# Gated recurrence and low-rank mixer: a half-word sign step, the second chunk's gates by a ratio, and a re-planned order

## The chip, the cores and the metric

One Trainium2 chip, one core. The metric is the device time of one execution in microseconds (us); lower is better. The kernel before was timed in three runs: 546.83, 547.58 and 550.12 us, median 547.58 us. Separately, one execution was profiled; it took 550.73 us, and the durations quoted below come from that one.

## What is computed

Two blocks follow each other. The first is a recurrence with complex gates over 768 steps, for 4 batches and 8 heads of 48 channels; the second is a mixer over the 384 columns that the heads make together. Cut to what matters:

```python
mag = np.sqrt(a_re * a_re + a_im * a_im)
scale = np.minimum(mag, 0.999) / (mag + 1e-06)
a_re_n, a_im_n = (a_re * scale, a_im * scale)
for t in range(S):
    ar, ai = (a_re_n[:, :, t, :, None], a_im_n[:, :, t, :, None])
    new_re = ar * S_re - ai * S_im
    new_im = ar * S_im + ai * S_re
    kv = np.einsum('bhd,bhe->bhde', k[:, :, t], v[:, :, t])
    S_re, S_im = (new_re + kv, new_im)
    y[:, :, t] = np.einsum('bhd,bhde->bhe', q[:, :, t], S_re)

xt = x.transpose(0, 2, 1)               # x: y of all heads, 384 columns
u = x + (xt @ U @ V).transpose(0, 2, 1)
out = u + np.maximum(u @ w_ch1, 0.0) @ w_ch2
```

The four weight arrays (`U`, `V`, `w_ch1`, `w_ch2`) come as 64-bit floats; everything else is 32-bit. The kernel turns the weights into 32-bit floats itself.

## The kernel before, in words

**Tiling.** The 4 x 768 steps are 24 chunks of 128 steps. Chunks go in pairs, called groups, for the gates (12 groups) and for the mixer. The gates of a chunk become a log magnitude (`GL`) and an angle (`gate`, then `F`, in turns). A matmul with a triangle of ones sums them along the chunk (tile `es ps` for magnitudes, `ph` for angles); exponentials (`es`) and sines (`cs`) of the sums weigh `q` and `k` (`qk`, then `QKC`); transposes (`tr`), products (`inner`, `dk`, `y`) and a running state (`GM`, `G`) give the output of the chunk (`xo`). The mixer then takes `rank`, `mixed`, the first weight product (`up` for the first two pairs, `few` with fewer products for the others) and the second (`down`).

**Gates.** `magnitudes_of(lo, hi)` works on chunks lo to hi-1. The first group is done chunk by chunk (parts (0,1) and (1,2)), every other group as one part of two chunks. There are two ways. The long one squares both parts on ACT, adds the squares with a clamp (L660), keeps the larger square (L661), makes two checks of the angle's range into `bad` (L663), and takes the logarithm of the sum and, apart from that, of the larger square. The other, `ratio_of` (L685), takes the logarithm of the real part (after L689), its reciprocal by an exponential, the ratio of imaginary to real part, its square with the check `wide` (L693), and finds the log magnitude from the ratio (L697, L700). The angle comes from the ratio in both. Before, the test is on the group: `g >= RATIO` with `RATIO = 1`, so both chunks of group 0 take the long way.

**Weights.** `single` (L558) converts one piece of 128 x 768 weights: 12 such pieces and one of 384 columns (`U` and `V`). A piece lies in one of two `raw` buffers as pairs of 32-bit words. Five steps follow: the high word read as a float and scaled (into the weight tile), the low word scaled to an integer of three bits (into a `cx` buffer), a shift left by 3 (L589), an integer add of the two (L445, the group `w<-w,stage`), and the sign, ORed in from the high word by a two-operand step (L591). For the first six pieces all five are on DVE; for the later ones the two scalings are on ACT (L439, `w<-stage` and `stage<-stage`). `raw` and `cx` are both views of a tile named `stage` in the profile.

**Order.** Every operation is recorded in a plan. `ORDER` is a written-out list of operation numbers; the program is issued in that order, so each engine's queue and each DMA queue (SP's, POOL's) holds its own operations in the order of that list. `SPARE` puts matmuls on the identity ahead of named operations (L1421, L1425). An assertion demands that an operation comes after what it needs and that a buffer is free. Loads are issued by SP in that order too, so a load waits in SP's queue for its buffer and everything behind it waits too. At the end a flag is read, and where a check has failed a slow general version runs; it does not run with these inputs.

Lines L436, L439, L442 and L445 are helpers: table load, activation, multiply, add.

## Time and profile before

| | |
|---|---|
| three timed runs | 546.83, 547.58, 550.12 us (median 547.58) |
| the profiled execution, its own time | 550.73 us |
| its span, first to last instruction | 548.5 us |
| time outside the span | 2.2 us |
| ACT busy | 297.3 us (54%) |
| POOL busy | 32.0 us (6%) |
| moved by DMA | 39.92 MB, over half of it in the first 140 us |

PE is the matmul engine, PEld its weight loads, DVE, ACT and POOL the vector, scalar and general engines, SP the engine that issues most DMAs. A busy PE in this profile is one that has a matmul under way; ends of matmuls are modelled. A line of a group gives source line, engine, operation, tile written and read, shape, and count. The chain of waits is the chain of work that ended last, followed back from the last instruction.

### The profile page before, as it was taken

The numbers are of one execution on the slowest core, as the hardware profiler recorded it, in microseconds if no ns is written. First come the engines' busy times: TensorE is split into PE (matmuls) and PEld (weight loads), VectorE is DVE, ScalarE is ACT, GpSimd is POOL, SyncE is SP. The second block draws the span as 40 slices with busy tenths as digits, with TensorE's granted clock in tenths as the row PEclk, the third lists the DMA queues.
The fourth block names the chain that finished last, engine by engine and source line by source line (L and its number), as shares of the span: only waits on it lengthen the run. The fifth ranks groups of instructions, "written<-read, shape, count | busy, mean of one in ns | idle before, by whom it ended". The sixth has DMA issues, their size and how long they took to land.

```text
span 548.5 us, 16738 instructions
## 1 busy us (share of the span) xinstructions
PE 524.2 (96%) x7296; PEld 473.6 (86%) x7296; DVE 419.6 (77%) x819; ACT 297.3 (54%) x545; POOL 32.0 (6%) x61
## 2 busy tenths in 40 slices
PE   2889989999999999999999999999999999999996
PEld 1767776867899998999999889999999989999995
DVE  6999995999999987897896775788685635656452
ACT  6889986894586866657457644533654322011100
POOL 1000000000020001000101001000111000000020
PEclk9999997999999999999999999999999999999999
DMA  9689893753325550422343420220131000000021
GB/s 222 130 177 202 168 211 81 188 96 75 57 54 110 90 111 11 87 38 38 73 76 72 90 42 20 46 46 17 29 76 46 3 2 1 1 14 2 1 73 34
DMA packets 150688, 39.92 MB, mean 73 GB/s; under 512 B 145912, under 2 KB 147408, under 8 KB 150608
## 3 DMA queue, kind: packets, MB, share of 16 engines
q1 hardware_dynamic: 148400, 34.43, 32.1%
q0 software_dynamic: 2208, 4.35, 2.4%
q8 instruction: 59, 0.97, 0.8%
q14 instruction: 21, 0.17, 0.1%
HBM read 33.60 MB, written 4.76 MB: 70 GB/s over the span
## 4 chain that ended last, share of the span: by engine, by line
PE 82%; DVE 9%; ACT 4%; DMA 3%; issue 2%; SPq 0%; DVEq 0%; ACTq 0%; POOLq 0%
PE down L1270 28%; PE few L1138 23%; PE dk L895 4%; PE inner L875 4%; PE y L932 4%; PE tr L846 4%; PE y L924 2%; PE up L1026 2%; DMA gate<-F 2%; PE rank L968 2%; PE mixed L991 2%; ACT gate L439 1%; PE uTp L1009 1%; PE es ps L721 1%; PE es ps L725 1%
## 5 line engine op out<-in xcount | busy, mean ns | idle before, releaser
L1146 ACT COPY h<-few 128x512 f32<-128x512 f32 x60 | 34.7, 586 | 79.4 <-PE few L1138 79.2
L1270 PE MATMUL down<-w,h 128*128 128x192 f32 x396 | 72.6, 330 | 0.7 <-ACT h L439 0.7
L852 ACT COPY QK<-tr 112x512 f32<-112x512 f32 x96 | 51.4, 593 | 35.3 <-PE tr L846 35.2
L1270 PEld LDWEIGHTS down<-w,h 128*128 128x128 f32 x396 | 64.4, 190 | 2.9 <-ACT h L439 1.2
L445 DVE TENSOR_TENSOR xo<-down,xo 128x192 f32<-128x192 f32 (+1 forms) x79 | 29.9, 385 | 37.0 <-PE down L1270 36.7
L1138 PE MATMUL few<-extra,w 128*128 128x128 f32 x400 | 50.3, 276 | 0.0
L1138 PEld LDWEIGHTS few<-extra,w 128*128 128x128 f32 x400 | 47.7, 192 | 0.2
L445 DVE TENSOR_TENSOR h<-few,h 128x512 f32<-128x512 f32 x30 | 20.6, 689 | 34.5 <-PE few L1138 22.1
L439 ACT ACTIVATE gate<-gate 128x768 f32<-128x768 f32 (+1 forms) x52 | 40.7, 792 | 11.3 <-DVE wide L693 7.8
L1150 DVE CUSTOM_DVE_ANT_1 h<-few,h 128x512 f32<-128x512 f32 x60 | 39.7, 684 | 7.6 <-PE few L1138 7.1
L442 DVE TENSOR_TENSOR QKC<-qk,cs 128x768 f32<-128x768 f32 x48 | 44.8, 950 | 0.3
L1270 PE MATMUL down<-stage 128*128 128x192 f32 x198 | 38.4, 332 | 0.0
L1026 PE MATMUL up<-uT,w 128*128 128x256 f32 x144 | 35.5, 397 | 0.2 <-ACT extra L439 0.2
L1270 PEld LDWEIGHTS down<-stage 128*128 128x128 f32 x198 | 32.3, 190 | 2.2 <-issue 1.5
L1026 PEld LDWEIGHTS up<-uT,w 128*128 128x128 f32 x144 | 27.3, 195 | 6.5 <-ACT xo L943 1.2
L1138 PE MATMUL few<-gate,w 128*128 128x128 f32 x240 | 31.9, 277 | 0.0
L436 ACT ACT_TABLE_LOAD x24 | 30.8, 1283 | 1.1 <-PEq L1477 0.7
L1214 POOL DMA_DIRECT2D out_dram<-xo x32 | 19.6, 645 | 191.1 <-DVE xo L445 159.5
L771 POOL DMA_DIRECT2D gate<-F x15 | 12.1, 805 | 303.2 <-DVE F L794 166.2
L1138 PEld LDWEIGHTS few<-gate,w 128*128 128x128 f32 x240 | 29.2, 192 | 0.4 <-DVE gate L1110 0.2
L895 PE MATMUL dk<-VP,QKC 64*48 64x48 f32 (+1 forms) x1408 | 27.6, 217 | 1.1 <-issue 1.1
L846 PEld LDWEIGHTS tr<-ident,QKC 64*112 64x112 f32 x768 | 23.7, 130 | 5.5 <-issue 2.3
(166 smaller groups left out, 1089.3 us busy)
## 6 DMA issues: line engine op xcount, KB each, us to landing
stage<-in_moe_w_ch_dram SPq DMA_DIRECT2D x12, 768.0 KB, 4.7
gate<-in_a_re_dram SPq DMA_DIRECT2D x24, 192.0 KB, 4.6
gate<-in_a_im_dram SPq DMA_DIRECT2D x24, 192.0 KB, 3.4
qk<-in_k_dram SPq DMA_DIRECT2D x24, 192.0 KB, 4.8
qk<-in_q_dram SPq DMA_DIRECT2D x24, 192.0 KB, 3.1
VP<-in_v_dram SPq DMA_DIRECT2D x24, 192.0 KB, 4.5
out_dram<-xo POOLq DMA_DIRECT2D x12, 192.0 KB, 2.9
out_dram<-xo POOLq DMA_DIRECT2D x20, 96.0 KB, 2.2
```

The lines of the kernel that those rows point to most:

```text
L436: ACT(1.4, rank, lambda: nc.scalar.preload_act_table_set(name), writes=[TABLE])
L439: return nc.scalar.activation(out=o, in_=i, func=f, **kw)
L442: nc.vector.tensor_tensor(out=o, in0=a, in1=b, op=OP.mult)
L445: nc.vector.tensor_tensor(out=o, in0=a, in1=b, op=OP.add)
L846: nc.tensor.transpose(out=get(*ps[r])[0:DQ, h], in_=get(*qkc)[at, h].rearrange("p u d -> p (u d)")[:, 0:DQ], identity=ident[at, at], tile_ ...
L852: nc.scalar.copy(out=get(*QK)[:, u].rearrange("p (h t) -> p h t", t=CH)[:, :, r * HC:(r + 1) * HC], in_=get(*ps[r])[0:DQ])
L895: nc.tensor.matmul(out=get(*dk[r])[x:end, h], lhsT=get(*ks)[at, h, x // DP, 0:end - x], rhs=get(*VPi)[at, h], start=True, stop=True, tile_ ...
L1026: nc.tensor.matmul(out=get(*ps)[:, e], lhsT=w1[:, f, (ff + e) * 128:(ff + e + 1) * 128], rhs=get(*uT)[:, f], start=(f == 0), stop=(f == KD ...
L1138: nc.tensor.matmul(out=get(*ps)[:, q], lhsT=w()[:, q * 128:(q + 1) * 128], rhs=v[0](), start=(n == 0 and q == 0), stop=True, skip_group_ch ...
L1146: ACT(c_act(n3 * CH) - 0.045, RU, lambda i=i, k=k: nc.scalar.copy(out=at(i, k), in_=get(*ps)), [ps], [o])
L1150: DVE(c_dve(n3 * CH), RU, lambda i=i, k=k: nc.vector._custom_dve(dve_ops.TENSOR_ADD_SAT, out=at(i, k), in0=get(*ps), in1=at(i, k), s0=math ...
L1270: nc.tensor.matmul(out=get(*to)[:, part], lhsT=x(j), rhs=y[:, j], start=(first and j == 0), stop=(j == KH - 1), skip_group_check=not first)
```

## The change

Three things are changed, and nothing else.

**The sign of converted weights.** The two-operand step L591 is gone. In its place a one-operand step on 16-bit halves takes the top half of each high word, keeps its sign bit, and writes it to the upper half of the `cx` word. The low word's scaling writes the lower half of that word only. The integer add then brings in low bits and sign together. The step reads one half of every 8 bytes and writes one half of every 4.

```diff
-        for to_word, o_, i_, scale, at in ((False, lambda: o, lambda: hi().bitcast(FP), 2.0 ** -112, to),
-                                           (True, lambda: word(x()), lo, 2.0 ** -29, cx)):
+        limb = lambda a, u: a.bitcast(U16).rearrange("p (n u) -> p n u", u=2)[:, :, u]
+        top = lambda: get("raw", p)[:, 0:n].rearrange("p n two -> p (n two)").bitcast(U16).rearrange("p (n u) -> p n u", u=4)[:, :, 3]
+        for o_, i_, scale, at in ((lambda: o, lambda: hi().bitcast(FP), 2.0 ** -112, to), (lambda: limb(x(), 0), lo, 2.0 ** -29, cx + (0,))):
...
+        DVE(one, rank, lambda: nc.vector.tensor_scalar(out=limb(x(), 1), in0=top(), scalar1=0x8000, scalar2=None, op0=OP.bitwise_and),
+            [raw], [cx + (1,)])
         DVE(one, rank, lambda: nc.vector.tensor_scalar(out=b, in0=b, scalar1=3, scalar2=None, op0=OP.logical_shift_left), writes=[to])
         DVE(two, rank, lambda: add(word(o), word(o), word(x())), reads=[cx], writes=[to])
-        DVE(two, rank, lambda: nc.vector.scalar_tensor_tensor(out=b, in0=hi(), scalar=0x80000000, in1=b,
-                                                              op0=OP.bitwise_and, op1=OP.bitwise_or), reads=[raw], writes=[to])
```

**The second chunk's gates.** The test is on the part's first chunk, so chunk 1 takes `ratio_of`; chunk 0 alone keeps the long way, and `bad` has two columns fewer.

```diff
-    bad = singles.tile([128, 1 + 2 * GC], FP, name="bad")
+    bad = singles.tile([128, 1 + 2 * RATIO], FP, name="bad")
...
-            if g >= RATIO:
+            if lo >= RATIO:
                 ratio_of(lo, hi, t, R1, W, X, L, Y, AR, AI)
                 return
```

**The order.** `ORDER` is another list, of 2200 operations by a new numbering where there were 2203; the identity matmuls of `SPARE` keep their counts and their places (2, 10, 14 and 5). The multiset of PE, POOL and SP operations is the same in both kernels; their sequence is not. Lines of the changed kernel lie one or two lower than before (L591 is the new sign step there, L593 the shift).

## The prediction

> **What bounds the kernel now.** I read the totals first, then a table of busy time by stage, then the chain of waits, and only then single steps.

> ```profile
> span 548.5 us, 16738 instructions
> PE 524.2 (96%) x7296; PEld 473.6 (86%) x7296; DVE 419.6 (77%) x819; ACT 297.3 (54%) x545; POOL 32.0 (6%) x61
> ```

> PE is busy for 524.2 of 548.5 us, so at most 24.3 us of the span is time in which no matmul ran. The busy share alone does not say where that time lies; the table by stage does (columns: stretch, its length, busy us of PE, PEld, DVE, ACT, POOL with counts, granted PE clock, DMA share, GB/s).

> ```profile
> 0.00:20.00 20.00, 8.45 (x39) 6.10 (x40) 14.37 (x38) 13.46 (x25) 2.17 (x14) 1.00 0.90 204
> 20.00:40.00 20.00, 17.09 (x424) 14.40 (x422) 19.30 (x31) 18.08 (x33) 0.00 (x0) 1.00 0.74 150
> 40.00:60.00 20.00, 19.79 (x371) 15.64 (x365) 19.57 (x32) 18.91 (x34) 0.00 (x0) 1.00 0.90 199
> 60.00:80.00 20.00, 19.38 (x413) 15.28 (x413) 18.92 (x32) 19.38 (x35) 0.00 (x0) 1.00 1.03 199
> 80.00:100.00 20.00, 18.34 (x155) 12.38 (x155) 13.71 (x24) 13.85 (x24) 0.00 (x0) 0.83 0.48 121
> 100.00:120.00 20.00, 19.86 (x91) 14.28 (x90) 19.26 (x31) 16.88 (x27) 0.96 (x1) 1.00 0.69 140
> 120.00:140.00 20.00, 19.18 (x164) 13.98 (x163) 19.22 (x30) 11.29 (x18) 2.11 (x3) 1.00 0.42 78
> 200.00:250.00 50.00, 50.00 (x658) 45.64 (x653) 42.60 (x88) 31.61 (x59) 3.31 (x5) 1.00 0.24 46
> 500.00:548.00 48.00, 43.29 (x315) 42.59 (x313) 24.03 (x57) 3.88 (x8) 3.73 (x7) 0.98 0.09 31
> ```

> Three things are to be seen. From 140 us on PE has no gap worth naming (200 to 250 is full), and the last 4.7 us are the outputs leaving. Both parts of the change lie ahead of 140 us, where all weights are converted and the first gates made. There PE loses 11.55 us in the first 20 (it waits for the first gates), 2.91 in the next 20, then 0.21, 0.62, 1.66, 0.14 and 0.82. DVE is at 95 to 98% in the five stretches from 20 us on that have the full clock, ACT at 90 to 97% up to 80 us. So DVE work removed there is real, but PE has the same work as before, and only PE's gaps can be given back. What DVE saves beyond them is hidden behind PE.

> **The sign step.** Durations of one 128 x 768 step, and the pace of neighbours:

> ```profile
> L585 DVE TENSOR_SCALAR stage<-stage x6: 353/552/556, 12.1 to 56.5; 128x768 int32<-128x768 uint32 x5, 128x384 int32<-128x384 uint32 x1
> L589 DVE TENSOR_SCALAR w<-w 128x768 uint32<-128x768 uint32 x12 | 6.7, 554 | 2.9 <-ACT w L439 2.8
> L591 DVE SCALAR_TENSOR_TENSOR w<-stage,w x12: 948/954/967, 16.9 to 118.9; 128x768 uint32<-128x768 uint32 x12
> 12.05 0.55 DVE L585 TENSOR_SCALAR stage<-stage 128x768 int32<-128x768 uint32 x1
> 12.52 0.55 DVE L585 TENSOR_SCALAR w<-stage 128x768 f32<-128x768 f32 x1
> 118.00 1.82 DVE L591 SCALAR_TENSOR_TENSOR w<-stage,w 128x768 uint32<-128x768 uint32 x2
> SPq L572 <- DVE w L591: 26.9, 6, 9.2
> ```

> A two-operand step takes 0.954 us, a one-operand step 0.55; neighbours overlap, so what counts is the pace: 1.82 - 0.954 = 0.87 us against 12.52 - 12.05 = 0.47. Removed: 12 x 0.87 and one of 384 columns, about 0.47. Added: 12 x 0.47 and one of about 0.27. The saving on DVE is 10.9 - 5.9 = 5.0 us. No row shows a step that writes every other 16-bit half. Its bounds are the one-operand rows (0.47) and the two-operand row (0.87, no saving at all); below 0.47 I see no reason to go, since no row has a quicker step of 768 elements. I take 0.47, because L585 already reads one word of every 8 bytes and takes 0.552, the same as L589, which reads without gaps. The same doubt holds for the low word's scaling, which now writes halves: 0 to 0.4 us for each of the five whole pieces on DVE and 0.2 for the short one, 2.2 in all; I take 0.

> [...]

> The change also moves a buffer's release. SP's weight loads (L572) waited 26.9 us in all for L591, the last reader of `raw`. Now the last reader is the sign step, ahead of the integer add, and the loads start earlier, into a stretch where DMA is already at 0.90 to 1.03. PE is not waiting for these loads, so I count nothing; what it can do to PE is a rival.

> **The second chunk's gates.**

> ```profile
> 5.96 0.56 DVE L660 CUSTOM_DVE_ANT_0 GL<-gate 128x384 f32<-128x384 f32 x1 [0.23 <-ACT gate L439]
> 6.56 0.52 ACT L439 ACTIVATE GL<-GL 128x384 f32<-128x384 f32 x1 [0.62 <-DVE GL L660]
> 7.21 0.62 ACT L439 ACTIVATE gate<-GL,leps 128x384 f32<-128x384 f32 x1
> 7.86 0.36 DVE L671 TENSOR_SCALAR GL<-GL 128x384 f32<-128x384 f32 x1 [0.27 <-ACT gate L439]
> 11.11 0.56 DVE L445 TENSOR_TENSOR GL<-GL,gate 128x384 f32<-128x384 f32 x1 [0.25 <-ACT gate L439]
> 12.64 1.17 PE L725 MATMUL es ps<-GL,prefix_r 128*128 128x384 f32 x2
> 20.34 0.55 DVE L794 SCALAR_TENSOR_TENSOR F<-F,ph 128x384 f32<-128x384 f32 x1 [0.75 <-ACT F L439]
> 23.01 0.95 DVE L442 TENSOR_TENSOR qk<-qk,es 128x768 f32<-128x768 f32 x1
> 31.52 0.96 DVE L700 SCALAR_TENSOR_TENSOR GL<-GL,gate 128x768 f32<-128x768 f32 x1
> 32.62 1.53 PE L725 MATMUL es ps<-GL,prefix_r 128*128 128x384 f32 x4 [1.03 <-DVE GL L700]
> ```

> The ratio way has fewer steps but one long chain. Chunk 1's chain starts on DVE behind the step of 5.96, at about 6.43, and by these rows is 0.36 + 3 x 0.52 (logarithms) + 0.52 + 0.62 (exponentials) + 4 x 0.56 = 5.3 us; with ten hand-overs of 0.03 and some 0.3 for chunk 0's steps on the same engines it ends near 12.3. Before, the operand was there at 11.67, but its matmul started at 12.64, behind chunk 0's sum and the identity matmuls. So the longer chain is hidden, by 0.3 us; each us beyond that would move the table load, the angles and everything after by as much. Chunk 0's own add comes up to 0.3 us earlier, since two steps of chunk 1 no longer stand before it on DVE. ACT's new order (one more sine ahead of the second `F`) takes that back by 20.34. I count 0 here. Loads: the second half of `qk` for chunk 1 now stands behind two more gate loads and `VP`, some 0.6 MB, in SP's queue; 4.2 MB up to it at about 225 GB/s (204 over the first 20 us, which begin with 2 us of silence) lands near 20.6, 2.4 us ahead of its use at 23.01.

> **The other order.** From `F` at 20.34 to the end of L700 at 32.48 DVE is nearly full, and PE waits for that step (1.03 us at 32.62). Ahead of it the new order has one step of 0.47 less (L689, now before `F`), one sign of 0.87 less and one 384-column step of 0.27 less, and a shift and a `G` product of 0.47 each more: -0.7 us. The `G` product needs the totals, whose read-back now stands ahead of the next `qk` loads, so I add no wait.

> Then the small gaps: 0.21 + 0.62 + 0.14 + 0.82 = 1.79 us of PE in 40 to 80 and 100 to 140, while DVE is full and gets lighter. I take half: -0.9 us.

> One place gets tighter. From the third group of chunks on, an angle sum needs the previous `F` by way of a DMA that adds it:

> ```profile
> 125.37 1.11 PE L785 MATMUL ph<-GS,prefix_r 128*128 128x384 f32 x2
> 126.32 2.74 PE L1227 MATMUL down<-w,extra 128*128 128x384 f32 x8
> 128.99 1.14 PE L895 MATMUL dk<-VP,QKC 64*64 64x48 f32 x64
> 130.06 1.11 PE L846 MATMUL tr<-ident,QKC 64*112 64x64 f32 x32
> 131.10 2.86 PE L1026 MATMUL up<-uT,w 128*128 128x256 f32 x12
> 133.60 0.70 PE L785 MATMUL ph<-GS,prefix_r 128*128 128x384 f32 x2
> DMA to landing us min/median/max: 1.8/2.9/4.2
> ```

> Here 8.2 us lie between the two `ph`. In the new order half a block of `down` (1.3), three halves of a `tr` block (1.6), a block of `down` (2.6) and `dk` (1.1) lie between, with `ph` itself 7.4 us. If the chain still needs 8.2, PE waits 0.8; with the median landing, 1.1 us under the longest, it does not. I take +0.3.

> The sum: -0.7 - 0.9 + 0.3 = -1.3 us. The profiled execution (550.73: span 548.5 and 2.2 around it) would become 549.4; it stands 3.15 us above the median of the timed runs, and the same 1.3 us off 547.58 gives **546.3 us**.

> **The rivals.** The low clock in 80 to 100:

> ```profile
> 81.67 0.66 PE L924 MATMUL y<-VP,AT 64*64 64x48 f32 x11 [2.22 <-issue]
> 82.00:84.00 2.00, 2.00 (x43) 1.91 (x35) 2.00 (x3) 0.00 (x0) 0.00 (x0) 0.50 0.05 13
> 86.00:88.00 2.00, 2.00 (x6) 1.43 (x5) 0.97 (x2) 0.96 (x2) 0.00 (x0) 0.50 1.06 357
> 88.00:90.00 2.00, 2.00 (x14) 0.81 (x12) 0.54 (x1) 0.60 (x2) 0.00 (x0) 0.89 0.14 27
> ```

> PE stops for 2.22 us between two matmuls of one group, with nothing to wait for but its own instructions, right after the stretch with the fullest DMA; then its clock is 0.50 for 6 us, which costs 3.2 (20 us at 0.83 lose 3.4, less what fell into the stop). Price 5.4 us.

> *Faster:* with the loads spread otherwise, this stop does not come: 546.3 - 5.4 = 540.9. For it: it hangs on one moment of full DMA. Against: DMA has the same bytes to move, PE the same instructions, and the median may be without the stop already.

> *Slower than before:* earlier weight loads crowd one more stop of PE's instructions, or a wait of its own, at a place with a full DMA between 20 and 80 us. It decides from a stop of about 2 us, after which the clock halved here; waits of 1 us (32.62) left it at 1.00. 546.3 + 5.4 = 551.7.

> *Half words are slow:* sign steps at 0.87 and scalings 0.4 longer. The two gains go (+0.7 + 0.9), and up to 2.2 us of new DVE work in a stretch where DVE is full partly shows: 548 to 550, taken as 549. [...]

> *Nothing comes of it:* PE's gaps are of another kind and stay; 547.6.

> **How the numbers follow.** Forecast 0.50, the stop gone 0.19, one more stop 0.13, slow half words 0.10, nothing 0.08. About 1% (5.5 us) is what a measurement of this kernel can tell from no change, so the borders are 542.1 and 553.1. Faster takes the case of the stop gone and a tail: 0.20. Slower takes the upper part of one more stop (0.07) and bad ends of the others (0.03): 0.10. The rest, 0.70, is within. The range goes from 540.5, which leaves out the lower half of the case of the stop gone, to 551.8, which leaves out the upper half of that of one more stop: some 0.18 outside.

> **What would show it.** Right: sign steps at 0.55 us; the second group's `es ps` matmuls near 31.9; PE's gaps from 40 to 140 smaller while the rest of PE is as it was. Wrong: sign or low-word steps near 0.95; the second chunk's sum after 12.7; a clock under 1.00 in a new place, or none anywhere; gaps of PE behind 140 us, above all ahead of `ph`.

## The result, and the profile after

| | median of the runs | ratio to the kernel before, 95% interval |
|---|---|---|
| kernel before | 550.01 us (11 runs, 546.83 to 551.10) | |
| changed kernel | 545.70 us (11 runs, 544.20 to 547.76) | 0.9936 [0.9915, 0.9957] |

The change makes the kernel 0.64% faster. The forecast was 546.3 us, but that it came so near is luck: it took 1.3 us off 547.58, and the kernel before measures 550.01 over eleven runs. The steps that led to it fared worse than the number, as the experiments show. The profiled execution of the changed kernel took 544.20 us, that of the kernel before 550.73.

First the totals on the page of the changed kernel.

```profile
span 542.4 us, 16751 instructions
PE 520.9 (96%) x7296; PEld 473.8 (87%) x7296; DVE 414.9 (76%) x816; ACT 298.3 (55%) x544; POOL 31.9 (6%) x61
```

DVE lost 4.7 us of work (419.6 to 414.9), PE's busy time fell by 3.3 us although it has the same 7296 matmuls, and the time without a matmul fell from 24.3 to 21.5 us. Where, the table by stage says (columns as before the change: stretch, its length, busy us of PE, PEld, DVE, ACT and POOL, granted PE clock, DMA share, GB/s).

```profile
0.00:20.00 20.00, 9.24 (x36) 6.91 (x37) 11.09 (x33) 12.71 (x23) 1.99 (x14) 1.00 0.90 203
20.00:40.00 20.00, 17.08 (x413) 14.61 (x413) 19.57 (x33) 17.69 (x32) 0.00 (x0) 1.00 0.93 199
40.00:60.00 20.00, 19.76 (x354) 15.41 (x354) 18.94 (x32) 19.23 (x35) 0.00 (x0) 1.00 0.74 160
60.00:80.00 20.00, 19.73 (x452) 15.93 (x444) 18.49 (x29) 18.71 (x35) 0.00 (x0) 1.00 0.92 196
80.00:100.00 20.00, 18.31 (x180) 12.65 (x180) 15.11 (x31) 16.83 (x28) 0.96 (x1) 1.00 0.61 133
100.00:120.00 20.00, 20.00 (x78) 14.53 (x78) 19.93 (x30) 18.20 (x28) 0.77 (x1) 1.00 0.48 111
120.00:140.00 20.00, 19.45 (x260) 15.57 (x259) 18.37 (x29) 11.60 (x20) 0.75 (x1) 1.00 0.45 80
```

The row to look at is 80 to 100: the clock is 1.00 where it was 0.83. PE still stops there, in the same group of matmuls and between the same two of them (21 done, 11 to go), but for 1.78 us instead of 2.22. The timeline of PE, then the stretches around it:

```profile
81.51 0.43 PE L926 MATMUL y<-VP,AT 64*64 64x48 f32 x11 [1.78 <-issue]
```

```profile
78.00:80.00 2.00, 1.73 (x65) 1.55 (x61) 1.99 (x3) 1.75 (x5) 0.00 (x0) 1.00 1.33 217
80.00:82.00 2.00, 0.49 (x15) 0.44 (x17) 1.97 (x4) 1.72 (x3) 0.00 (x0) 1.00 0.93 126
82.00:84.00 2.00, 2.00 (x41) 1.32 (x42) 0.59 (x2) 0.91 (x4) 0.00 (x0) 1.00 0.06 14
84.00:86.00 2.00, 2.00 (x14) 1.59 (x17) 0.64 (x2) 0.84 (x2) 0.00 (x0) 1.00 0.13 12
```

So in these two executions the 6.1 us of difference in the span hold 0.4 us of a shorter stop and 3.2 us of a clock that did not fall. PE is also busy 0.8 us longer in the first 20 (9.24 us for 8.45), but that is no gain: twenty of the identity matmuls took 1.0 us longer there. Over all the profiles these twenty take 2.39 to 3.57 us, so this is a matter of the execution. The rows of the kernel before and of the changed kernel:

```profile
13.64 2.39 PE L1421 MATMUL ph<-ident 128*128 128x128 f32 x20
13.76 3.42 PE L1423 MATMUL ph<-ident 128*128 128x128 f32 x20
```

When PE comes to the stop it has run the same 1237 matmuls in both kernels, of the same kinds, and the changed kernel comes there later: at 79.73 us (81.51 - 1.78) for 79.45 (81.67 - 2.22). All that is gained lies behind that point. Of it, 1.0 us is between 300 and 350, where the changed kernel has no gap and the kernel before had this stop of PE's instructions:

```profile
315.22 0.78 PE L895 MATMUL dk<-VP,QKC 64*48 64x48 f32 x21 [0.89 <-issue]
```

The rest, 1.8 us, is in smaller pieces, 0.4 of it in PE's gaps from 100 to 140.

The clock is not kept in every execution: of the changed kernel's eleven timed runs five have a mean clock of 0.997 or more and take 544.20 to 544.74 us, six have 0.996 and take 545.70 to 547.76.

Now the steps. The groups of the converted weights on DVE and ACT in the changed kernel (after the bar: busy us, mean ns of one), and the timeline rows of the gates:

```profile
L591 DVE TENSOR_SCALAR stage<-stage 128x768 uint16<-128x768 uint16 x12 | 7.2, 601 | 0.4 <-DMA stage<-in_moe_w_ch_dram 0.4
L587 DVE TENSOR_SCALAR stage<-stage 128x768 uint16<-128x768 uint32 x5 | 3.0, 609 | 0.0
L440 ACT ACTIVATE stage<-stage 128x768 uint16<-128x768 uint32 x7 | 7.5, 1070 | 0.0
```

```profile
11.70 0.56 DVE L702 SCALAR_TENSOR_TENSOR GL<-GL,gate 128x384 f32<-128x384 f32 x1 [0.76 <-ACT gate L440]
12.41 1.55 PE L727 MATMUL es ps<-GL,prefix_r 128*128 128x384 f32 x2
18.95 0.60 DVE L591 TENSOR_SCALAR stage<-stage 128x768 uint16<-128x768 uint16 x1
19.43 0.55 DVE L691 TENSOR_SCALAR GL<-gate 128x768 f32<-128x768 f32 x1
21.32 0.55 DVE L796 SCALAR_TENSOR_TENSOR F<-F,ph 128x384 f32<-128x384 f32 x1
32.12 0.96 DVE L702 SCALAR_TENSOR_TENSOR GL<-GL,gate 128x768 f32<-128x768 f32 x1 [0.21 <-ACT gate L440]
33.23 1.21 PE L727 MATMUL es ps<-GL,prefix_r 128*128 128x384 f32 x3 [0.87 <-DVE GL L702]
```

A sign step on halves takes 0.601 us, where the two-operand step took 0.954. The second chunk's operand is there at 11.70 + 0.56 = 12.26 us. The second group's sum starts at 33.23 us, 0.6 us later than before.

### The profile page after: what moved, and what is told of

Read it like the earlier page. It is cut to its first block, busy times and chain, and to the rows that moved or that the text cites. A ratio compares the mean times of both kernels' runs of the same rounds, so it can differ in the third digit from the quotient of the medians.

```text
span 542.4 us, 16751 instructions
## 1 busy us (share of the span) xinstructions
PE 520.9 (96%) x7296; PEld 473.8 (87%) x7296; DVE 414.9 (76%) x816; ACT 298.3 (55%) x544; POOL 31.9 (6%) x61
## 4 chain that ended last, share of the span: by engine, by line
PE 75%; DMA 1%; DVE 0%; issue 0%
PE down L1272 29%; PE few L1140 25%; PE inner L877 3%; PE dk L897 3%; PE y L934 3%; PE tr L848 3%; PE y L926 2%; PE mixed L993 1%; PE rank L970 1%; PE uTp L1011 1%; PE up L1028 1%; PE ph L787 1%; PE es ps L723 1%; DMA gate<-F 1%; DVE xo L446 0%; DVE extra L1193 0%
## 5 line engine op out<-in xcount | busy, mean ns | idle before, releaser
L440 ACT ACTIVATE gate<-gate 128x768 f32<-128x768 f32 (+1 forms) x50 | 39.6, 797 | 16.4 <-DVE wide L695 12.8
L1028 PE MATMUL up<-uT,w 128*128 128x256 f32 x144 | 33.6, 384 | 0.5 <-DVE xo L446 0.5
L848 PE MATMUL tr<-ident,QKC 64*112 64x64 f32 x768 | 27.9, 219 | 1.3 <-DVE QKC L443 0.8
```

Source lines behind the costliest of these rows:

```text
L440: return nc.scalar.activation(out=o, in_=i, func=f, **kw)
L848: nc.tensor.transpose(out=get(*ps[r])[0:DQ, h], in_=get(*qkc)[at, h].rearrange("p u d -> p (u d)")[:, 0:DQ], identity=ident[at, at], tile_ ...
L1028: nc.tensor.matmul(out=get(*ps)[:, e], lhsT=w1[:, f, (ff + e) * 128:(ff + e + 1) * 128], rhs=get(*uT)[:, f], start=(f == 0), stop=(f == KD ...
```

## The experiments

Three questions were put. Which of the three parts carries the gain? Is the stop near 80 us made by the loads, and what is it worth? Which of the sign steps count? Each kernel was timed beside the kernel before on the same chip. "Places" are places in `ORDER`; line numbers in the rows are those of each kernel's own text. Theory A was put anew as results came, so each expectation says what it means by it.

**The old sign step in the new order.** The old conversion comes back for all thirteen pieces (its low-word step too, which writes whole words), with the two-operand step ahead of the add. Of a piece's two places for sign and shift the earlier went to the shift, the later to the sign; where the shift's operand is written only after the earlier place, both stand at the later one.

```diff
-        DVE(one, rank, lambda: nc.vector.tensor_scalar(out=limb(x(), 1), in0=top(), scalar1=0x8000, scalar2=None, op0=OP.bitwise_and),
-            [raw], [cx + (1,)])
         DVE(one, rank, lambda: nc.vector.tensor_scalar(out=b, in0=b, scalar1=3, scalar2=None, op0=OP.logical_shift_left), writes=[to])
+        DVE(two, rank, lambda: nc.vector.scalar_tensor_tensor(out=b, in0=hi(), scalar=0x80000000, in1=b,
+                                                              op0=OP.bitwise_and, op1=OP.bitwise_or), reads=[raw], writes=[to])
         DVE(two, rank, lambda: add(word(o), word(o), word(x())), reads=[cx], writes=[to])
```

> The changed kernel with the old sign step (two operands, 32 bits, 0.95 us) in the places of the new steps; ratio way and order stay as changed. Theory A (the gain is the stop of TensorE's instructions near 80 us: 2.22 us with the clock at 0.50 for 6 us before, 1.78 us with the clock kept after): the time follows that stop alone. If the stop here stays under about 2 us and the clock in 82 to 88 is 1.00, the ratio to the kernel before is 0.992 to 0.996; if the clock is 0.50 there, 0.998 to 1.001. TensorE's gaps outside 78 to 90 change by less than 1 us. Theory B (the gain is VectorE's 5 us, passed on through TensorE's gaps): 1.000 whatever the clock does, with gaps of TensorE up by 2 us or more between 20 and 140 us. Theory C (the other order alone makes the gain): 0.993.

Measured: 553.82 us, 1.0087 [1.0064, 1.0109]. All three theories had less. Part of it is an artefact of the experiment: a later run shows where one shift was put too early.

**The long way for the second chunk in the new order.**

```diff
-            if lo >= RATIO:
+            if g >= RATIO:
```

> The changed kernel with the second chunk's gates made the long way again; sign step and order of all else stay as changed. Theory A: 0.992 to 0.996 with the clock kept at 1.00 behind the stop near 80 us, 0.998 to 1.001 with 0.50. Theory B: 0.993, since the sign step is there. Theory C: 0.993. A fourth theory (the ratio way makes the gain at the start): 0.998 to 1.000 with the first 20 us losing about 0.8 us of TensorE's work. By the prediction's sum the ratio way is worth 0 (hidden by 0.3 us).

Measured: 545.44 us, 0.9931 [0.9904, 0.9958], against 0.9936 with the ratio way. The ratio way is worth nothing that these runs can tell, as the prediction had it. Its six runs again go with the clock, from 543.11 us at 1.000 to 548.29 at 0.993.

**The order alone**, with both edits undone:

> The old sign step and the long way for the second chunk, in the changed kernel's order of everything else. Theory A: as the stop near 80 us goes, 0.992 to 0.996 or 0.998 to 1.001. Theory B: 1.000 to 1.002, VectorE has its 5 us back. Theory C: 0.993.

Measured: 553.92 us, 1.0090 [1.0066, 1.0113]. As it stands the order brings no gain by itself, against theory C; but the same artefact is in it.

**The sign step alone**, in the order before; the new step stands right ahead of the add:

```diff
-    8, ... 9, 10,      # first piece: shift, add, old sign step
+    9, ... 8, 10,      # shift, new sign step, add
```

> The kernel before with the new sign step on 16-bit halves, put right ahead of the integer add; the rest of its order and the long way for the second chunk stay. Sign steps take 0.60 us (as in the changed kernel) and VectorE is 4 to 5 us less busy in the first 140 us. Theory A: the time follows the stop near 80 us; weight loads and arrival there hardly move, so most likely 0.998 to 1.001 with the clock at 0.50 behind it, 0.992 to 0.996 if the clock is kept. Theory B: 0.993. Theory C: 1.000.

Measured: 550.14 us, 1.0031 [1.0011, 1.0051]. Theory B is refuted: DVE has 3.5 us less to do (416.1 us busy) and the kernel is no faster. The profiled execution was the fastest of its twelve (547.27 us), and it shows one of the places where the saved time goes. Issues by SP and POOL, then DVE and PE:

```profile
96.25 0.37 SPq L558 DMA_DIRECT2D stage<-in_moe_w_ch_dram  x1
97.96 0.96 POOL L758 DMA_DIRECT2D gate<-F  x1 [90.40 <-DVE F L781]
102.61 0.36 DVE L766 CAST GS<-gate 128x384 fp32r<-128x384 f32 x1 [2.21 <-DMA gate<-F]
104.21 0.61 PE L772 MATMUL ph<-GS,prefix_r 128*128 128x384 f32 x2 [1.09 <-DVE extra L1059]
```

The same place in the kernel before:

```profile
100.46 0.96 POOL L771 DMA_DIRECT2D gate<-F  x1 [92.72 <-DVE F L794]
101.08 0.37 SPq L572 DMA_DIRECT2D stage<-in_moe_w_ch_dram  x1
103.49 0.36 DVE L779 CAST GS<-gate 128x384 fp32r<-128x384 f32 x1
```

The new step frees `raw` sooner, so SP issues the next weight load 1.7 us ahead of POOL's small angle DMA, where it was 0.6 us behind it; two loads of 192 KB (at 96.67 and 97.66 us) go ahead of it too, which were behind it before. The small DMA now takes 4.65 us from its issue to its use (3.03 before), DVE stands still for 2.21 us, and the step that PE needs is behind it in DVE's queue. What DVE saved is spent waiting here. That the loads make the small DMA late is read from these two traces; no run tested it by itself. A weight load ahead is not enough: in the changed kernel one goes 2.25 us ahead (94.41 us, the small DMA at 96.66), with neither of the two 192 KB loads, and the small DMA is used after 2.71 us.

**Both parts in the old order**, the ratio steps in the places of the long way's:

> The kernel before with both parts (new sign step, ratio way for the second chunk) and its own order elsewhere; the chunk's steps stand in the places of its old ones. So far: the order alone 1.009, the sign alone 1.003, sign and order 0.993. Theory A (what counts is how VectorE's steps and the order fit: each order has its own places where TensorE waits, and the sign step gains only in the new one): 1.001 to 1.005, like the sign alone, the ratio way adding 0 or making the first 15 us worse by up to 0.3 us. Theory B (the two parts together gain, whatever the order): 0.993 to 0.996.

Measured: 552.90 us, 1.0059 [1.0031, 1.0086]. Theory A, a little worse than expected. The first gates ended 0.6 us later than before in this arrangement (PE waited 11.0 us for them, 10.4 before), so the extra 0.3% says nothing about the ratio way.

**Loads moved away from the stop, kernel before.** Two gate loads (635 and 634, 192 KB each) behind the value load 683:

```diff
-    635, 632, 55, ... 634, 605, ... 64, 683, 66,
+    632, 55, ... 605, ... 64, 683, 635, 634, 66,
```

> The kernel before, with two gate loads of 192 KB each (a_im of the fifth group, not used before about 95 us) issued behind the value load of 84 us instead of at 75 to 77 us, so that some 0.4 MB less stand in the DMA queues when TensorE reaches 79.5 us. Theory A (TensorE's stop there is its instructions waiting behind full DMA, and the clock drop follows from the length of the stop): the stop shrinks from 2.22 us to under 1.8, the clock in 82 to 88 stays at 1.00, ratio 0.991 to 0.995. Rival (the stop or the clock drop hangs on something else, a power limit or the work itself): stop and clock as before, 0.998 to 1.002.

Measured: 548.74 us, 0.9970 [0.9945, 0.9996]. Less than theory A wanted.

```profile
82.16 0.43 PE L909 MATMUL y<-VP,AT 64*64 64x48 f32 x11 [1.95 <-issue]
```

```profile
80.00:82.00 2.00, 0.22 (x13) 0.09 (x5) 1.86 (x3) 1.60 (x5) 0.00 (x0) 1.00 0.08 12
84.00:86.00 2.00, 2.00 (x10) 0.72 (x3) 0.93 (x2) 1.95 (x5) 0.00 (x0) 0.50 0.27 29
```

The stop became 1.95 us and the clock still fell. And DMA was nearly idle (0.08) through most of the stop, so full DMA is not all of its cause.

**The same in the changed kernel.** The value load 680 and the gate load 632 behind the weight load 64:

```diff
-    383, 680, 335, ... 440, 632, 57, ... 64, 618, ... 631, 611,
+    383, 335, ... 440, 57, ... 64, 680, 618, ... 631, 632, 611,
```

> The changed kernel, with one value load and one gate load of 192 KB each (issued at 66 and 78 us) moved behind the weight load of 85 us. Theory A: the stop near 80 us shrinks from 1.78 us to 0 to 1.3, and no timed run has the clock drop behind it (all at 0.998 or more): ratio 0.987 to 0.992, 1 to 3 us faster than the changed kernel. Rival (loads do not matter there): 0.993 to 0.994, with half of the runs at a mean clock of 0.996.

Measured: 544.15 us, 0.9904 [0.9863, 0.9945]; six of the seven runs have a clock of 0.997 or more.

```profile
80.66 0.69 PE L911 MATMUL y<-VP,AT 64*64 64x48 f32 x32
```

```profile
80.00:82.00 2.00, 2.00 (x82) 1.89 (x80) 1.99 (x4) 1.78 (x5) 0.00 (x0) 1.00 0.02 4
82.00:84.00 2.00, 2.00 (x28) 1.25 (x23) 1.93 (x4) 1.97 (x5) 0.00 (x0) 1.00 0.03 8
```

Here the group runs through in one piece (x32): DMA was all but idle (0.02) when PE came to the place near 81 us, and no stop is left. The interval still overlaps that of the changed kernel, which did not run beside it; the last run below settles that the loads are worth something.

**Loads moved towards the stop, changed kernel.** Key load 679 and value load 704 ahead of it:

```diff
-    703, 702, 171, ... 619, 704, 494, 679, 778,
+    703, 702, 679, 704, 171, ... 619, 494, 778,
```

> The changed kernel, with one more key load and one more value load of 192 KB each issued ahead of the stop near 80 us (at about 76 to 78 us) instead of at 85 to 86. Theory A: the stop grows from 1.78 us to 2.5 to 3.5, the clock is 0.50 for some 6 us behind it in nearly all runs (mean clock 0.993 or less): ratio 0.997 to 1.003. Rival: 0.993 to 0.994.

Measured: 546.53 us, 0.9939 [0.9910, 0.9968], the changed kernel's own ratio. The stop was 1.82 us, with the clock fallen behind it, not 2.5 to 3.5: 384 KB more in front of PE's instructions did not hold them up longer. Theory A missed here.

**The first weight's seven pieces, and the second weight's six, with the old steps:**

```diff
+        if p < 7:
+            # the old conversion steps; in the second kernel: if p >= 7
...
+        else:
+            # the new ones
```

> The changed kernel with the old sign and low-word steps for the seven pieces of the first weight alone (VectorE's sign steps up to about 62 us). With all thirteen back TensorE waited 3.1 us for AT near 66 us and its clock fell behind that; ratio 1.009. Theory A (VectorE, late by the sign steps ahead of 66 us, makes that wait, and the wait the clock drop): the same wait of 2 to 3.1 us with the drop, 1.004 to 1.009. Rival (each of the thirteen steps costs its share, 8 us over 13, wherever it is): 1.001 to 1.002.

Measured: 550.40 us, 1.0033 [1.0013, 1.0053].

```profile
63.15 1.03 DVE L576 TENSOR_SCALAR w<-w 128x768 uint32<-128x768 uint32 x2 [3.01 <-ACT w L425]
67.41 0.68 PE L924 MATMUL y<-VP,AT 64*64 64x48 f32 x32 [3.12 <-DVE AT L878]
```

```profile
65.00:70.00 5.00, 2.27 (x65) 2.10 (x66) 4.96 (x8) 0.92 (x3) 0.00 (x0) 0.91 0.93 244
70.00:75.00 5.00, 5.00 (x18) 3.79 (x17) 3.99 (x8) 4.48 (x10) 0.00 (x0) 0.75 0.87 136
```

This is the artefact. DVE is not late here by its load: it stands for 3.01 us at the shift of the seventh piece, which had come into the earlier place of the sign step and needs that piece's scaling by ACT. The new sign step needs only the loaded piece. PE then waits 3.12 us, and the clock of the next 10 us costs 5 x 0.09 + 5 x 0.25 = 1.7 us: together 4.8 us; this kernel is 5.0 us slower than the changed one beside it. But that is not the whole balance. The stop near 80 us (1.78 us in the first profile of the changed kernel) is not there: the group at 85.82 us runs through. In its place PE waits in all some 2 us longer at smaller places, the longest this one:

```profile
32.68 1.13 PE L895 MATMUL dk<-VP,QKC 64*64 64x48 f32 x60 [0.85 <-DVE G L431]
```

So the first seven sign steps may cost some 2 us beside the artefact; whether it is they or their places is not shown.

> The changed kernel with the old sign and low-word steps for the six pieces of the second weight alone (sign steps from about 63 us on). Theory A: no wait for AT near 66 us, the stop near 80 us as in the changed kernel: 0.993 to 0.997. Rival: six steps of thirteen give back their share: 1.000 to 1.001.

Measured: 550.19 us, 1.0021 [0.9996, 1.0045]. In these six pieces DVE stands at a shift no longer than in the changed kernel (2.24 us for ACT at 86.75 us, 2.25 there), so the artefact is not in them. Theory A was wrong: they cost 4.8 us against the changed kernel beside them (545.41).

```profile
64.88 0.68 PE L924 MATMUL y<-VP,AT 64*64 64x48 f32 x32 [1.22 <-ACT extra L425]
83.24 0.43 PE L924 MATMUL y<-VP,AT 64*64 64x48 f32 x11 [1.27 <-issue]
104.00 0.69 PE L1066 MATMUL fix<-V,more 32*128 32x256 f32 x2 [0.51 <-DVE extra L1072]
```

```profile
84.00:86.00 2.00, 2.00 (x34) 0.94 (x30) 0.51 (x1) 1.02 (x4) 0.00 (x0) 0.61 0.03 8
86.00:88.00 2.00, 2.00 (x9) 1.44 (x6) 1.22 (x2) 0.72 (x1) 0.00 (x0) 0.54 0.00 0
102.00:104.00 2.00, 1.43 (x8) 0.59 (x4) 1.95 (x4) 0.32 (x1) 0.00 (x0) 1.00 0.40 144
104.00:106.00 2.00, 2.00 (x6) 1.42 (x7) 1.76 (x4) 1.98 (x3) 0.00 (x0) 0.73 0.76 94
106.00:108.00 2.00, 2.00 (x7) 1.53 (x6) 1.97 (x4) 1.26 (x3) 0.00 (x0) 0.50 0.78 301
108.00:110.00 2.00, 2.00 (x10) 1.75 (x9) 1.97 (x4) 1.32 (x3) 0.00 (x0) 0.92 0.00 0
```

DVE is late for `fix` near 103, a stretch with few matmuls, and the clock falls behind a wait of only 0.51 us: 1.7 us over the last three rows (2 x 0.27 + 2 x 0.50 + 2 x 0.08). The order-alone kernel shows the same wait and a drop behind it, the changed kernel neither. Nor does the changed kernel, in either profile, have the wait of 1.22 us for ACT at 64.88. With 0.51 and 1.7 it makes 3.4 us; the rest of the 4.8 us was not located. The drop at 84 to 88 us is no difference that the old steps make: the second profile of the changed kernel, below, has it too.

**The changed kernel once more, and the long way with the loads moved:**

> The changed kernel as it is, beside the others. 0.9936 as before (0.991 to 0.996); its runs fall in two groups, at a mean clock of 0.999 near 544.4 us and at 0.996 near 546.8.

Measured: 545.41 us, 0.9935 [0.9914, 0.9957]. The profiled execution took 548.49 us; here the stop is as long as before the change, and the clock falls:

```profile
83.06 0.43 PE L911 MATMUL y<-VP,AT 64*64 64x48 f32 x11 [2.25 <-issue]
```

```profile
84.00:86.00 2.00, 2.00 (x28) 0.93 (x24) 0.00 (x0) 1.03 (x4) 0.00 (x0) 0.51 0.04 8
86.00:88.00 2.00, 2.00 (x9) 1.49 (x6) 0.65 (x2) 0.70 (x1) 0.00 (x0) 0.64 0.23 23
```

So 1.78 or 2.25 us, clock kept or not, is a matter of the execution. Nor can the clock be the main thing that the change gains: here the median of the runs' mean clocks is 0.997 for both kernels, and the changed one is still 4.0 us faster by the medians (545.41 for 549.37). Where these 4.0 us lie is not shown, since the only profile of the kernel before is one with a low clock.

> The changed kernel with the second chunk's gates made the long way and with the value load of 66 us and the gate load of 78 us behind the weight load of 85 us. The first alone gave 0.9931 against the changed kernel's 0.9936, the second 0.9904. Theory A (the ratio way is worth nothing, the stop near 80 us costs its length and at times the clock): stop under 1.3 us, clock kept, 0.988 to 0.993. Rival (the 1.5 us of the later loads were chance): 0.993 to 0.994.

Measured: 543.72 us, 0.9903 [0.9882, 0.9923]. Every one of its six runs (543.50 to 544.21) is below every one of the seven of the changed kernel beside them (544.90 to 548.49), and all have a clock of 0.998 or more. The stop is 1.38 us in its profile. So later loads are worth about 1.7 us, with the ratio way or without it.

**What the stop waits for.** The question whether the loads make the stop can be answered in part from the traces. They have a DMA queue called "instruction", which moves 16 KB at a time (q8 of the changed kernel: 59 packets, 0.97 MB). In each of the eleven profiles with this stop, one such load lands shortly before: PE goes on 1.25 to 1.58 us after it. In the kernel before it lands at 80.27 us and PE goes on at 81.67; in the changed kernel at 80.05 and 81.51; with the loads moved in the kernel before, at 80.81 and 82.16. In the three profiles where PE all but runs through, it goes on 1.27 to 1.53 us after the landing as well (in the changed kernel with the loads moved at 80.99, the load landing at 79.46): there the load came in time. So, as far as these fourteen profiles show, the stop is PE waiting for its own instructions, and how long it is depends on when PE comes there and when the load lands. This also fits the stop that the nearly idle DMA (0.08) did not explain: its load had landed 1.35 us before its end. Whether the other loads delay this one, or by how much, no run shows.

## Why the prediction was right, and where it was wrong

The time was 0.6 us off, well inside the range, but by luck. The forecast was a change of -1.3 us, taken off 547.58, the median of three runs. Over eleven runs the kernel before stands at 550.01, and the change is -3.5 us by the ratio (-4.3 by the medians), about three times the forecast. Of the sum's three terms one held in part, and most of what was gained comes from places that the sum left alone.

- **What bounds the kernel:** held in part. Ahead of 140 us PE's gaps decide; DVE's own time does not, which the sign step alone in the old order shows best. But not all that can be given back lies there: in the first two profiles 1.0 us came from a stop at 315 us, where the prediction saw no gap worth naming. Such late stops also vary: the second profile of the changed kernel has one of 0.8 us near 176.
- **Sign steps, pace 0.47, saving 5.0 us:** nearly. One takes 0.601 us and its neighbour starts 0.48 us later (18.95 to 19.43). Writing halves slows the low-word step too: on DVE, where the prediction took 0, to 0.609 us from 0.552, and on ACT, which it did not price, to 1.070 from 0.918 (row below, of the kernel before), 7 x 0.15 = 1.1 us.

```profile
L439 ACT ACTIVATE stage<-stage 128x768 int32<-128x768 uint32 x7 | 6.4, 918 | 0.3 <-DMA stage<-in_moe_w_ch_dram 0.3
```

- **Second chunk, 0:** held. Its chain ends at 12.26 us against 12.3 forecast, its sum starts at 12.41, and undoing it changes nothing that the runs can tell.
- **The second group's sum, -0.7:** failed, +0.6 (33.23 for 32.62). The step counted from `F` at 20.34 as if that stood still. In the new order `F` comes at 21.32, behind conversion steps put ahead of it, and L702 waits 0.21 us for ACT. The count of moved steps began too late in DVE's queue. At the stop near 80 us, where both kernels have run the same matmuls, the changed one is 0.3 us behind.
- **Half of the small gaps, -0.9:** in part. In 40 to 80 and 100 to 140 they are 0.24 + 0.27 + 0.00 + 0.55 = 1.06 us for 1.79. But 0.27 of these, and 0.55 of those before, are the beginning of the stop, which the prediction had counted among the small gaps (78 to 80 has 1.73 us of PE, before 1.45). Without it 1.24 became 0.79: -0.45, nearly all of it behind 100 us.
- **The angle chain, +0.3:** not seen. Two `ph` lie 7.3 us apart there, and PE does not wait for them:

```profile
122.26 0.61 PE L787 MATMUL ph<-GS,prefix_r 128*128 128x384 f32 x2
129.52 0.61 PE L787 MATMUL ph<-GS,prefix_r 128*128 128x384 f32 x2
```

- **The stop, kept as it was:** half held. It stays at its place, but how long it is and whether the clock falls varies between executions of one kernel. The profiled execution of before drew the dear case, that of after the cheap one; for it the sum gave 549.4 us and 544.2 came.
- **The faster rival, the stop gone, 540.9:** the mechanism is real, the price was too high. Moved loads, which took it away in one kernel and shortened it to 1.38 us in another, gave about 1.7 us; about half of the changed kernel's runs do without the drop already.
- **The slower rival, earlier weight loads that make a wait of their own:** this is what the sign step does in the old order (2.21 us of DVE, 1.09 of PE, for one), as far as two traces show it. In the new order PE has no such wait.
- **Slow half words, 549:** refuted by 0.601 us.

The deeper fault is that the prediction added up what each part relieves. The parts are not additive. The sign step costs 0.3% in the old order and gains in the new one: its six last pieces alone make 0.9% there. The order alone measured 1.009; less the artefact of 4.8 us, estimated from the run with seven pieces, it would stand near 549 us, about where the kernel before is. But in its profile the stop near 80 us is only 0.42 us, and without the artefact some of it could come back. So what exactly the order is worth alone stays open: the same kernels with the shift in its own place were not run.

## What to carry to other kernels

A cheaper step is worth what its queue does next: here, by the traces, an earlier buffer release sent large loads ahead of a small DMA, and the saved time turned into a wait until the order was made anew. When a part is undone for a test in a finely ordered kernel, look whether its steps stand where their operands are ready, or the test measures that instead. More busy time of an engine in a stretch is not yet a gain: look when both kernels have done the same work. And take more than one profile before explaining 1% by one stop: the same stop cost this kernel 1.8 us in one execution and 2.3 us and a halved clock in the next.

## What was not expected of the hardware

Ahead of the last matmul the clock drops to 0.50 thirteen times in all the profiles. Every drop lasts about 3.4 or 6.8 us (in the second profile of the changed kernel from 84.0 to 87.4, in the kernel before from 81.6 to 88.4). Where one profile has two drops, they start a multiple of 3.41 us apart: 84.4 and 104.9 us with the second weight's old steps (6 times), 67.4 and 108.4 with all the old steps (12 times), 68.4 and 105.9 with the order alone (11 times). In the kernel before, the drop behind the last matmul starts at 545.83 us, 464.2 us (136 times) after the one at 81.62. Counted on in steps of 464.2 / 136 = 3.413 us from the start of a drop, points follow that are estimates. In the profile of the changed kernel that kept the clock the only drop is the one behind the last matmul, from 541.55 us; 135 steps before it, at an estimated 80.75 us, such a point lies within the stop of 1.78 us, 1.02 us after its start and 0.76 before its end. The stop of 1.27 us that did not keep the clock lies, by the drop that starts at 84.4, between two such points (an estimated 81.0, and 84.4 us). Whether the clock is set at these points, and how much idle time makes it fall, is not shown: with the second weight's old steps it fell after 0.57 us of idle PE from 102 to 104 us, around the wait of 0.51.
